# Output products of a gated feed-forward kernel: h as the stationary operand and the output weights as the streamed one

## The chip, the cores and the metric

One core of a Trainium2 chip runs the kernel. The metric is the device time of one execution in microseconds (us). Its engines are TensorE (PE, matrix products; its weight loads are listed apart as PEld), VectorE (DVE), ScalarE (ACT), GpSimd (POOL) and SyncE (SP, which here only issues DMAs).

## The reference

Two stages follow each other. The first is a causal convolution over 7 taps whose weights are a softmax and differ by token and head; the second is a gated feed-forward layer. Tokens: 4 x 4096; channels: 192 in 8 heads of 24; hidden width: 1536.

```python
w = softmax(weight_gen, axis=-1)                      # (4, 4096, 8, 7)
x_unf = windows of 7 tokens of x, zeros ahead         # (4, 4096, 7, 8, 24)
x = einsum('bshk,bskhg->bshg', w, x_unf).reshape(16384, 192)
gate = 1 / (1 + exp(-(x @ w_gate)))                   # 192 -> 1536
out = (gate * (x @ w_val)) @ w_out                    # 1536 -> 192, float32
```

## The kernel before

**Precision.** PE works on fp32r operands, which hold fewer bits than fp32. Each operand is therefore kept as a rounded part and a rest: W as hi and lo, h as hh and hl, the convolved x as two planes. A product is made of three: hi x hi, lo x hi and hi x lo.

**Tiling.** The 16,384 tokens are 32 blocks (n) of 512. The hidden width is 12 slices (f) of 128. A *unit* is one slice of one block. The first slices of blocks 0 and 1 are cut into two units of 256 tokens (table `APART`), so that PE can begin with half a block.

**PE's order.** The array is split into an upper and a lower half of 64 rows (`UP`, `LOW`), which run two matmuls beside each other; a product that contracts 128 or 192 channels is made of such halves. A unit's period (`period`) has 14 slots, each one matmul of 512 columns in the lower half paired with one in the upper half. Gate (lower half, 9 matmuls, `G`) and value (upper half, 9, `V`) belong to unit s. The output products (`out_jobs`: 5 matmuls in each half) belong to the unit three periods earlier (`LAG`); the upper half makes its five in slots 2 to 6, the lower half in slots 9 to 13. The output weights are stationary and h streams, 512 tokens at a time: three products for output channels 0 to 127 into one bank (`ph`), two for channels 128 to 191, hi and lo side by side as 128 columns, into another (`pt`). `ph` and `pt` have two banks each, which alternate between blocks; gate and value have the other four of the eight PSUM banks. The output leaves transposed, channels by tokens, and is turned on the host side of the return.

**Turns.** Both halves add into the same bank, one after the other. Where a bank passes from one half to the other, `emit` puts a GpSimd memset of one cell (`seen`) between the last matmul of one and the first of the other.

**Other engines in a unit.** ACT takes the sigmoid of the gate (L1050), DVE multiplies by the value (L1053), ACT rounds h to hh (L1056), DVE subtracts for hl (L1059). At the end of a block `evac` copies `ph` (ACT, L1108), copies the upper half of `pt` (ACT, L1111), adds it to the lower half (DVE, L1114) and stores both (SP).

**Opening.** Nothing can be multiplied before the first softmax, the spreading of its weights over partitions (L637), the tap products (DVE, L796) and their sum. For the first half block, the heads of the second half block and those of block 1's first half, that sum is made on PE by an identity matrix (L718, table `SUMS`), elsewhere on DVE (L704). ACT then rounds (L826, L872), DVE subtracts for the rest (L829, L875), and ACT copies the halves crosswise (`As`, `T`). The weights of each slice are loaded, put together and split by `convert`: ACT, DVE, ACT, then two DVE subtractions (L472). Units of blocks 0 and 1 alternate in turns of six slices: block 0, f 0 to 5; block 1, f 0 to 5; block 0, f 6 to 11; block 1, f 6 to 11.

**The order.** All operations are recorded with a modelled duration, a due time and the buffers that they take; a list scheduler (`Plan.order`) sets the order on each engine. Its first operations are not planned but listed by number (`FIRST`). Engines then run their queues in order and wait by semaphores. Where the plan sees PE idle early on, matmuls on a blank tile are put in (`idle`, `between`).

Of the kernel before, what the change touches and what calls it, by code (L numbers as in the profile page):

```python
# [62 lines left out]
class Plan:  # L63
# [26 lines left out]
    def op(self, engs, fn, deps=(), alloc=(), uses=(), due=INF, table=None, nbytes=0, late=0.0, after=(), lag=None, port=True, more=0.0, lead=0.0, hold=None, tail=0.0):  # L90
# [12 lines left out]
        o.name = name  # L103
# [27 lines left out]
    def order(self):  # L131
# [17 lines left out]
        table, dma_free = None, 0.0  # L149
# [11 lines left out]
        def slots(o):  # L161

            got, when = [], 0.0
            for p, _ in o.alloc:
                best = None
                for b in self.places[p]:
# [104 lines left out]
def conv_gated_ffn(ctx: ExitStack, tc: tile.TileContext, xt, wg, wcat, outT):  # L271
# [30 lines left out]
    SUMS = {(0, 0): ("ph", "pt"), (0, M2): ("ph", None), (1, 0): ("ph", None)}  # L302
    APART = {0: (4, HALVES), 1: (3, HALVES)}
# [31 lines left out]
    place("ev", 2, [P, N], F32)  # L335
    place("osb", 2, [P, N], F32)
# [3 lines left out]
    for name, a, z in (("gv", 0, 4), ("ph", 4, 6), ("pt", 6, 8)):  # L340
        plan.place(name, [bank[:, i, :] for i in range(a, z)])
# [36 lines left out]
    LAG, SKIP = 3, 0  # L378
# [14 lines left out]
    def out_unit(s):  # L393

        if s < SKIP:
            return s - LAG + 1
        return s - LAG if s > SKIP else -1

    def out_period(u):
        return u + LAG - 1 if u + LAG - 1 < SKIP else u + LAG  # L400

    for s in range(len(units) + LAG):
        for i, slots in enumerate((2, 5, 2, 5) if out_unit(s) >= 0 else (0, 0, 9, 0)):
            _, _, a, z = units[min(s, len(units) - 1)]
            t += slots * slot(z - a)
            due[s, i] = t

    def due_block(n):
        return due[out_period(last_unit[n]), 3]
# [29 lines left out]
    LO = CT + R  # L439
    conv_op, selected = {}, {}  # L440

    def convert(f, due=INF):
# [4 lines left out]
        def ld(buf, e):  # L447
# [6 lines left out]
            {"sp": SP}, ld, [selected.get(f)], after=[prev.get("ld")], nbytes=P * CT * 8 * RAW, due=due  # L454
# [15 lines left out]
        def lows(a, z, to):  # L470
            def f_lo(buf, e):
                nc.vector.tensor_tensor(  # L472
                    out=W[f][:, to : to + z - a], in0=buf[E][:, a:z],
                    in1=W[f][:, a:z].bitcast(F32), op=ALU.subtract,
                )

            return f_lo

        o_top = op({"act": act(CT) + 0.06}, f_top, [o_ld], alloc=[("ch", X)])
        o_va = op({"dve": dve(CT) + 0.035}, f_value, [o_ld, o_top], alloc=[("ce", E)], uses=[X])  # L480
        o_hi = op({"act": act(CT)}, f_hi, [o_va], uses=[E])
        o_lo = [
            op({"dve": dve(z - a)}, lows(a, z, to), [o_hi], uses=[E])
            for a, z, to in ((0, CB + P, LO), (CB + P, CT, CT))
        ]
        conv_op[f] = dict(ld=o_ld, done=[o_hi] + o_lo)


# [743 lines left out]
```

## Time and profile before

| | us |
|---|---|
| median of 3 runs | 1255.74 (1255.38 to 1256.42) |
| profiled execution | 1255.93 |
| its span, first to last instruction | 1254.2 |
| PE busy | 1244.5 (99%) |
| PE weight loads busy | 1103.6 (88%) |
| DVE busy | 976.5 (78%) |
| ACT busy | 597.0 (48%) |
| POOL busy | 135.2 (11%) |

Busy times are unions over the span; of matmuls that overlap, as pairs on the two halves of the array do, each has its own duration in the tables of groups. A matmul's listed duration holds the time in which its last column drains, so the step from one start to the next, not the duration, says what it costs a full queue. Register, branch, semaphore and DMA-issuing instructions are not counted as busy.

### The profile page before, as it was taken

Reading aid. Unit: us, or ns where it says so; the run is one execution under the profiler, and the core shown is the slowest. Engines: PE = TensorE matmul, PEld = TensorE weight load, DVE = VectorE, ACT = ScalarE, POOL = GpSimd, SP = SyncE. Lnnn points to the kernel's source line nnn. Section 1 sums busy time; section 2 is a strip of 40 time slices with the busy share of each in tenths; the row PEclk is TensorE's granted clock in tenths of the full one; section 3 lists DMA queues with packets and bytes.
Section 4 is the critical chain, followed back from the end, with each engine's and each line's share of the span. In section 5 each row is a group of like instructions: output and inputs, shape, how many; then the busy total and the mean of one; then the engine's idle time right before and its main releaser. Section 6 shows DMA issues by size and latency. Waiting matters only on the chain.

```text
span 1254.2 us, 29144 instructions
## 1 busy us (share of the span) xinstructions
PE 1244.5 (99%) x11047; PEld 1103.6 (88%) x11047; DVE 976.5 (78%) x1444; ACT 597.0 (48%) x1016; POOL 135.2 (11%) x1498
## 2 busy tenths in 40 slices
PE   8999999999999999999999999999999999999998
PEld 7988888888888888888888888888888888888887
DVE  8999998898977688776778767688676887767743
ACT  6866555554534444444444444444344444444443
POOL 0111111111111111111111111111111111111110
PEclk9999999999999999999999999999999999999999
DMA  9765539445272743529344282652727335293100
GB/s 252 234 160 131 140 85 230 116 120 140 72 176 72 175 105 82 127 71 202 77 118 110 63 197 73 140 121 58 168 72 182 97 80 129 72 204 75 39 14 14
DMA packets 48988, 150.33 MB, mean 120 GB/s; under 512 B 6544, under 2 KB 19280, under 8 KB 48848
## 3 DMA queue, kind: packets, MB, share of 16 engines
q1 hardware_dynamic: 48704, 148.22, 49.0%
q8 instruction: 86, 1.41, 0.5%
q14 instruction: 54, 0.44, 0.1%
q10 hardware_dynamic: 144, 0.26, 0.1%
HBM read 110.24 MB, written 16.20 MB: 101 GB/s over the span
## 4 chain that ended last, share of the span: by engine, by line
PE 97%; DVE 1%; DMA 1%; issue 0%; ACT 0%; SPq 0%
PE bank L971 97%; PE bank L718 1%; DMA wb<-ws 1%; DMA ws<-w 0%; DVE prod L770 0%; DVE sg L1053 0%; DVE prod L704 0%; DVE hl L1059 0%; DVE m L516 0%; DVE eye L600 0%; DVE w L523 0%; DVE osb L1114 0%; DVE sel L605 0%; DVE W L472 0%; SPq L663 0%
## 5 line engine op out<-in xcount | busy, mean ns | idle before, releaser
L971 PE MATMUL bank<-hh,W 64*128 64x512 f32 (+2 forms) x2337 | 769.5, 383 | 0.0
L971 PE MATMUL bank<-As,W 64*128 64x512 f32 (+1 forms) x2346 | 646.5, 383 | 0.0
L971 PE MATMUL bank<-T,W 64*128 64x512 f32 (+1 forms) x2346 | 645.8, 382 | 0.0
L971 PE MATMUL bank<-hl,W 64*128 64x512 f32 (+1 forms) x1558 | 594.4, 382 | 0.2 <-DVE hl L1059 0.2
L971 PE MATMUL bank<-A,W 64*128 64x512 f32 (+1 forms) x2346 | 479.8, 382 | 0.0
L1056 ACT CAST hh<-sg 128x512 fp32r<-128x512 f32 (+1 forms) x391 | 239.9, 614 | 490.7 <-DVE sg L1053 490.4
L971 PEld LDWEIGHTS bank<-hh,W 64*128 64x128 f32 (+1 forms) x2337 | 428.5, 184 | 29.9 <-POOL seen L967 0.4
L971 PEld LDWEIGHTS bank<-T,W 64*128 64x128 f32 x2346 | 426.8, 184 | 29.6 <-ACT T L895 0.3
L971 PEld LDWEIGHTS bank<-As,W 64*128 64x128 f32 x2346 | 427.1, 184 | 29.2
L1053 DVE TENSOR_TENSOR sg<-bank,sg 128x512 f32<-128x512 f32 (+1 forms) x391 | 265.1, 678 | 168.1 <-PE bank L971 167.9
L1059 DVE TENSOR_TENSOR hl<-sg,hh 128x512 fp32r<-128x512 f32 (+1 forms) x391 | 265.4, 679 | 97.0 <-ACT hh L1056 94.5
L971 PEld LDWEIGHTS bank<-A,W 64*128 64x128 f32 x2346 | 298.3, 184 | 30.0 <-issue 0.3
L971 PEld LDWEIGHTS bank<-hl,W 64*128 64x128 f32 x1558 | 286.8, 184 | 20.0 <-DVE hl L1059 0.4
L1050 ACT ACTIVATE sg<-bank 128x512 f32<-128x512 f32 (+1 forms) x391 | 231.5, 592 | 116.0 <-PE bank L971 112.4
L967 POOL MEMSET seen<- 1x1 f32 x1490 | 133.5, 90 | 1110.2 <-PE bank L971 1108.1
L770 DVE TENSOR_TENSOR prod<-x,wb 128x1024 f32<-128x1024 f32 x126 | 136.4, 1084 | 0.9 <-DMA wb<-ws 0.7
L704 DVE TENSOR_TENSOR prod<-prod,prod 128x1024 f32<-128x1024 f32 (+2 forms) x94 | 104.2, 1109 | 0.0
L770 DVE TENSOR_TENSOR prod<-xt,wt 128x1024 f32<-128x1024 f32 (+1 forms) x66 | 68.7, 1042 | 0.0
L704 DVE TENSOR_TENSOR acc<-prod 128x512 f32<-128x512 f32 (+2 forms) x64 | 34.3, 536 | 0.1
L826 ACT CAST A<-acc 128x512 fp32r<-128x512 f32 (+1 forms) x31 | 19.0, 612 | 17.8 <-DVE acc L704 17.8
L1114 DVE TENSOR_TENSOR osb<-bank,ev 64x512 f32<-64x512 f32 x32 | 21.5, 671 | 1.4 <-ACT ev L1111 1.4
L704 DVE TENSOR_TENSOR prod<-prod 128x512 f32<-128x512 f32 (+1 forms) x34 | 22.5, 661 | 0.0
(52 smaller groups left out, 307.5 us busy)
## 6 DMA issues: line engine op xcount, KB each, us to landing
wb<-ws SPq DMA_DIRECT2D x60, 896.0 KB, 11.9
wt<-ws SPq DMA_DIRECT2D x30, 896.0 KB, 8.9
As<-A SPq DMA_DIRECT2D x56, 256.0 KB, 3.7
out<-osb SPq DMA_DIRECT2D x31, 256.0 KB, 2.4
x<-in_x SPq DMA_DIRECT2D x30, 259.0 KB, 9.5
T<-T SPq DMA_DIRECT2D x56, 128.0 KB, 4.1
raw<-in_w SPq DMA_DIRECT2D x12, 575.8 KB, 6.0
out<-osb SPq DMA_DIRECT2D x32, 128.0 KB, 2.5
```

Of the source, the lines that this page charges most:

```text
L704: nc.vector.tensor_tensor(out=dst(buf), in0=a(buf), in1=b(buf), op=ALU.add)
L718: nc.tensor.matmul(out(buf), eye, flat(buf, i, j - k, j - k + 1), start=j == 0, stop=j == K - 1,)
L770: nc.vector.tensor_tensor(out=dst.rearrange("p (k j t) -> p k j t", k=z - k, t=L), in0=sliding(buf[X][:, k : k + cols], z - k, [[L, cols / ...
L826: nc.scalar.copy(buf[A][:, 0, all_], buf[ACC][:, :C])
L967: turn = nc.gpsimd.memset(seen, 0.0)
L971: ins = nc.tensor.matmul(buf[dst][:, c:d], w, m, start=start, stop=stop)
L1050: nc.scalar.activation(out=buf[k["sg"]][:, a:z], in_=buf[k["g"]][:, a:z], func=AF.Sigmoid)
L1053: nc.vector.tensor_tensor(out=buf[k["sg"]][:, a:z], in0=buf[k["v"]][:, a:z], in1=buf[k["sg"]][:, a:z], op=ALU.mult)
L1056: nc.scalar.copy(buf[k["hh"]][:, a:z], buf[k["sg"]][:, a:z])
L1059: ENG[e].tensor_tensor(out=buf[k["hl"]][:, a:z], in0=buf[k["sg"]][:, a:z], in1=buf[k["hh"]][:, a:z].bitcast(F32), op=ALU.subtract)
L1114: nc.vector.tensor_tensor(out=buf[OT][LOW, :N], in0=buf[PT][LOW, :N], in1=buf[EV][LOW, :N], op=ALU.add)
```

## The change

Output products: h is now the stationary operand, 128 tokens at a time, and the output weights stream. For each 128 tokens (j = 0 to 3) and each half, hh is multiplied by hi and lo side by side (2 x 192 = 384 columns) and hl by hi (192 columns). One bank for each j (`po`) takes the sums, channels of hi in its first 192 columns and of lo in the next. All four banks belong to one block at a time. The two halves' matmuls are listed in the order of their modelled starts (`streams`) instead of in pairs; in the upper half output products follow 4 of the value's matmuls (`HEAD`), in the lower half all 9 of the gate's.

At a block's end ACT copies each bank's 384 columns, DVE adds hi and lo columns of all four in one operation, and one DMA stores tokens by channels. The last block is copied, added and stored bank by bank.

Around it: the slices of blocks 0 and 1 are no longer taken in turns; block 0 is in halves for f 0 to 5, block 1 for f 0 to 3. Only block 0's sums are made on PE. Where they are, PE also takes the rest (a product with a negative identity, `f_rest`), and ACT rounds it, instead of a DVE subtraction; for the heads and tail of block 0's second half, PE makes the crosswise turn too (`f_turn`). Each tap of a PE sum is an operation of its own. The weights' lo part is one DVE subtraction of 576 columns instead of two. Units 0 and 1 make their products with A and As before unit 0 makes those with T. `FIRST` is a new and longer list (its numbers are left out here).

```diff
-    LAG, SKIP = 3, 0
+    LAG, HEAD = 3, 4
-    SUMS = {(0, 0): ("ph", "pt"), (0, M2): ("ph", None), (1, 0): ("ph", None)}
-    APART = {0: (4, HALVES), 1: (3, HALVES)}
+    SUMS = {(0, 0): ("po", "po"), (0, M2): ("po", None)}
+    APART = {0: (6, HALVES), 1: (4, HALVES)}
+    TURNS = {(0, M2)}
...
-    place("ev", 2, [P, N], F32)
-    place("osb", 2, [P, N], F32)
+    place("ev", 1, [P, N // P, 2 * D], F32)
-    for name, a, z in (("gv", 0, 4), ("ph", 4, 6), ("pt", 6, 8)):
+    for name, a, z in (("gv", 0, 4), ("po", 4, 8)):
...
-    TURN = 6
-    spans = [(n, f, g) for f, g in ((0, TURN), (TURN, NF)) for n in range(2)]
-    for n, first, end in spans + [(n, 0, NF) for n in range(2, NB)]:
+    for n in range(NB):
         apart, cuts_ = parts(n)
-        units += [(n, f, a, z) for a, z in cuts_ for f in range(first, min(apart, end))]
-        units += [(n, f, 0, N) for f in range(max(first, apart), end)]
+        units += [(n, f, a, z) for a, z in cuts_ for f in range(apart)]
+        units += [(n, f, 0, N) for f in range(apart, NF)]
...
+            def f_rest(buf, e):
+                nc.tensor.matmul(
+                    buf[ACC][:, :n_], minus, buf[X][:, 0, here], start=False, stop=True, skip_group_check=True
+                )
...
+                if summed:
+                    nc.scalar.copy(buf[X][:, 1, here], buf[ACC][:, :n_])
+                else:
+                    nc.vector.tensor_tensor(
+                        out=buf[X][:, 1, here], in0=buf[ACC][:, :n_],
+                        in1=buf[X][:, 0, here].bitcast(F32), op=ALU.subtract,
+                    )
...
+                def f_turn(buf, e):
+                    opened.append(buf[B])
+                    nc.tensor.matmul(
+                        buf[B][:, :W2], turn_, buf[X][:, :, here], start=True, stop=True
+                    )
...
-    def out_jobs(u, r, head_first, last=False):
+    def out_jobs(u, r, last=False):
...
+        for j in range(a // P, z // P):
+            jobs.append((k["po"][j], (f, 2, j), k["hh"], rows, None, (0, 2 * D), f == 0 and r == 1, False))
+            jobs.append((k["po"][j], (f, 1, j), k["hl"], rows, None, (0, D), False, last))
...
+                if dst[0] == "po":
+                    f_, parts_, j = w
+                    w = buf[t][rows, j * P : (j + 1) * P]
+                    m = W[f_][rows].rearrange("p (w c) -> p w c", w=2)[:, :parts_, CB:]
+                    if parts_ == 1:
+                        m = m[:, 0]
...
+    def streams(low, up):
+        tops, out = [0.0, 0.0], []
+        todo = [list(low), list(up)]
+        while todo[0] or todo[1]:
+            i = 0 if not todo[1] or (todo[0] and tops[0] <= tops[1]) else 1
+            job = todo[i].pop(0)
+            out.append((tops[i], job))
+            tops[i] += cost(job)
+        return out, max(tops)
...
+            jobs, took = streams(G + low, V[:HEAD] + up + V[HEAD:])
...
+            if not fo:
+                cuts_ += [at[j[1:4]] for j in up[2::2]]
             if last:
-                evac(no, [c])
+                cuts_ += [at[j[1:4]] + 1 for j in low[1::2]]
...
+                    alloc=([("gv", g) for g in gv] if not i else []) + [("po", d) for d in new],
...
+            def f_copy(buf, e, j=j, PO=PO):
+                nc.scalar.copy(buf[EV][:, j], buf[PO][:, : 2 * D])
...
+            o = op(
+                {"act": act(D if end else 2 * D, True) + 0.12}, f_low if end else f_copy, [d], alloc=alloc,
+                uses=[PO] + ([EV] if j else []), after=copies[-1:], due=t - 4 + j if not end else t, lag=1,
+            )
...
+        if not end:
+            store(slice(0, N // P), [add(slice(0, N // P), copies)], "sp")
...
+    for s in range(2):
+        period(s, (0, 1))
     for s in range(len(units)):
-        period(s)
+        period(s, (2,) if s < 2 else (0, 1, 2))
```

## Rows read from the trace of the kernel before

**Rows 1.** The page, its first part: busy us (share of the span) xinstructions.
```profile
PE 1244.5 (99%) x11047; PEld 1103.6 (88%) x11047; DVE 976.5 (78%) x1444; ACT 597.0 (48%) x1016; POOL 135.2 (11%) x1498
```

**Rows 2.** Chain that ended last, in order of time: start us, us, what.
```profile
27.02 3.22 PE bank L718 x14
...
45.42 1203.58 PE bank L971 x10636
```

**Rows 3.** Timeline, steady stretch: start us, us, engine line operation out<-in.
```profile
700.03 0.63 PE L971 MATMUL bank<-A,W 64*128 64x512 f32 x4
...
700.49 0.39 PE L971 MATMUL bank<-As,W 64*128 64x512 f32 x1
700.49 0.18 PEld L971 LDWEIGHTS bank<-As,W 64*128 64x128 f32 x1
...
706.38 0.63 PE L971 MATMUL bank<-A,W 64*128 64x512 f32 x4
```

**Rows 4.** Busy time by stretch; last three columns: PE clock, DMA share, GB/s.
```profile
0.00:50.00 50.00, 44.87 (x430) 41.12 (x432) 45.47 (x96) 35.69 (x81) 4.96 (x44) 1.00 0.89 254
...
300.00:500.00 200.00, 200.00 (x1768) 177.07 (x1766) 156.40 (x226) 92.42 (x153) 21.50 (x240) 1.00 0.47 111
```

**Rows 5.** Timeline of weight loads, opening; xcount loads in one piece.
```profile
8.30 0.97 PEld L637 LDWEIGHTS bank<-w,sel 128*128 128x128 f32 x8 [0.90 <-DVE w L573]
...
17.18 1.64 PEld L718 LDWEIGHTS bank<-prod,eye 128*128 128x128 f32 x14 [0.83 <-DVE prod L796]
...
26.95 2.89 PEld L718 LDWEIGHTS bank<-prod,eye 128*128 128x128 f32 x14
```

**Rows 6.** Timeline where PE starts again after a wait.
```profile
44.95 0.42 DVE L1059 TENSOR_TENSOR hl<-sg,hh 128x256 fp32r<-128x256 f32 x1
...
45.42 0.18 PEld L971 LDWEIGHTS bank<-hl,W 64*128 64x128 f32 x1 [0.42 <-DVE hl L1059]
...
45.42 0.18 PEld L971 LDWEIGHTS bank<-As,W 64*128 64x128 f32 x1
...
45.53 0.19 PEld L971 LDWEIGHTS bank<-hh,W 64*128 64x128 f32 x1
45.53 0.19 PEld L971 LDWEIGHTS bank<-T,W 64*128 64x128 f32 x1
```

**Rows 7.** Timeline of half-array products with 256 columns, upper half.
```profile
30.75 0.28 PE L971 MATMUL bank<-hl,W 64*128 64x256 f32 x1
...
30.87 0.28 PE L971 MATMUL bank<-hh,W 64*128 64x256 f32 x1
```

**Rows 8.** Groups by line: xcount | busy us, mean ns | idle before.
```profile
L967 POOL MEMSET seen<- 1x1 f32 x1490 | 133.5, 90 | 1110.2 <-PE bank L971 1108.1
...
L1056 ACT CAST hh<-sg 128x512 fp32r<-128x512 f32 x377 | 234.3, 621 | 488.5 <-DVE sg L1053 488.4
L1050 ACT ACTIVATE sg<-bank 128x512 f32<-128x512 f32 x377 | 226.2, 600 | 115.4 <-PE bank L971 111.9
L1108 ACT COPY osb<-bank 128x512 f32<-128x512 f32 x32 | 18.8, 587 | 0.6
...
L826 ACT CAST A<-bank 128x256 fp32r<-128x256 f32 x3 | 1.1, 371 | 1.8 <-PE bank L718 1.8
...
L704 DVE TENSOR_TENSOR prod<-prod,prod 128x768 f32<-128x768 f32 x31 | 29.5, 951 | 0.0
```

**Rows 9.** Timeline of one turn: the last product and GpSimd's write.
```profile
301.57 0.39 PE L971 MATMUL bank<-hl,W 64*128 64x512 f32 x1
...
302.08 0.09 POOL L967 MEMSET seen<- 1x1 f32 x1 [0.36 <-PE bank L971]
```

**Rows 10.** Timeline of the opening, ACT, DVE and PE.
```profile
15.46 0.37 ACT L826 CAST A<-bank 128x256 fp32r<-128x256 f32 x1 [0.63 <-PE bank L718]
...
17.51 0.42 DVE L829 TENSOR_TENSOR A<-bank,A 128x256 fp32r<-128x256 f32 x1
...
18.94 0.62 PE L971 MATMUL bank<-A,W 64*128 64x256 f32 x6
```

More of the change, by code (lines that the diff above doesn't have):

```diff
@@ L88, in place, with op @@
         self.places[name] = [dict(buf=b, key=None) for b in bufs]
-    def op(self, engs, fn, deps=(), alloc=(), uses=(), due=INF, table=None, nbytes=0, late=0.0, after=(), lag=None, port=True, more=0.0, lead=0.0, hold=None, tail=0.0):
+    def op(self, engs, fn, deps=(), alloc=(), uses=(), due=INF, table=None, nbytes=0, late=0.0, after=(), lag=None, port=True, more=0.0, lead=0.0, hold=None, tail=0.0, fixed=False):
         keys = [k for _, k in alloc] + list(uses)
@@ L408, in due_block @@
     def due_block(n):
-        return due[out_period(last_unit[n]), 3]
+        return due[last_unit[n] + LAG, 3]
     x_op = {}
@@ L627, in idle, with spread @@
             )
-    def spread(key, chunks, sel, deps):
-        keys_ = [(key, i) for i in range(chunks // 2)]
+    def spread(key, chunks, sel, half):
+        keys_ = [(key, half, i) for i in range(chunks // 2)]
+        deps = [soft[0]["spread"][half]]
         def f(buf, e):
@@ L996, in conv_gated_ffn, with cost, pe, period @@
     u_op = {}
-    def pe(slots, deps, **kw):
+    def cost(job):
+        return slot(job[5][1] - job[5][0])
+    def pe(jobs, deps, took=None, **kw):
         last_pe[0] = op(
-            {"pe": sum(slot(max(j[5][1] - j[5][0] for j in p if j)) for p in slots)}, emit(slots), deps + [last_pe[0]], **kw
+            {"pe": sum(map(cost, jobs)) if took is None else took}, emit(jobs), deps + [last_pe[0]], **kw
         )
         return last_pe[0]
-    def period(s):
+    def streams(low, up):
[7 more added lines that the diff above has]
+        return out, max(tops)
+    def period(s, which=(0, 1, 2)):
         u = out_unit(s)
@@ L1025, in period @@
                 b.fill = between(s, not i)
+            if 2 not in which:
+                return
         else:
             last = fo == NF - 1
[L1028 to L1031 removed]
+            up, low = out_jobs(u, 1), out_jobs(u, 0, last)
             gv = [k["g"], k["v"]]
[L1033 to L1036 removed]
@@ new lines, in period @@
+            done = {}
+            for i, (x, y) in enumerate(zip(cuts_, cuts_[1:])):
+                part = [j for _, j in jobs[x:y]]
+                mine = [j[0] for j in part if j[0][0] == "po"]
+                mine = list(dict.fromkeys(mine))
+                new = [j[0] for j in part if j[0][0] == "po" and j[6]]
+                o = pe(
+                    part, deps if not i else conv_op[fo]["done"] + u_op[u] if x == at[up[0][1:4]] else [],
+                    time[i + 1] - time[i],
+                    alloc=([("gv", g) for g in gv] if not i else []) + [("po", d) for d in new],
+                    uses=xs + (gv if i else []) + [d for d in mine if d not in new] + ([ko["hh"], ko["hl"]] if mine else []),
+                    due=due[s, 0 if not i else 1 if x < at[low[0][1:4]] else 3],
+                )
+                if i < 2:
+                    o.fill = between(s, not i)
+                if y == at[low[0][1:4]]:
+                    b = o
+                for d in mine:
+                    done[d] = o
@@ L1049, in f_sig @@
+            c = o
+            if last:
+                evac(no, [done[po(j)] for j in range(N // P)])
         def f_sig(buf, e):
@@ L1072, in ending @@
     def ending():
-        three = range(len(units) - LAG, len(units))
-        ks = [keys(u) for u in three]
-        po = [ks[0]["ph"], ks[0]["pt"]]
-        used = [[k["hh"], k["hl"]] for k in ks]
-        def jobs(u, part, stop=False):
-            out = out_jobs(u, 0, True)
-            out = out[:3] if part == "ph" else out[3:]
-            out = [j[:3] + (slice(0, P),) + j[4:7] + (False,) for j in out]
-            if stop:
-                out[-1] = out[-1][:7] + (True,)
-            return [(j,) for j in out]
@@ L1087, in side @@
-        def side(jobs, deps, used, at):
-            return pe(jobs, deps, uses=po + used, due=due[len(units) + at, 3])
-        cf = sum((conv_op[units[u][1]]["done"] for u in three), [])
-        x, y, z = three
-        side(
-            sum((jobs(u, part) for u in (x, y) for part in ("ph", "pt")), []),
-            cf + u_op[x] + u_op[y], used[0] + used[1], 1,
-        )
-        t = jobs(z, "pt", True)
-        side(t[:1], u_op[z][:1], used[2], 2)
-        t = side(t[1:], u_op[z], used[2], 2)
@@ new lines, in ending, with side @@
+        x, y, z = range(len(units) - LAG, len(units))
+        ks = [keys(u) for u in (x, y, z)]
+        po = ks[0]["po"]
+        cf = sum((conv_op[units[u][1]]["done"] for u in (x, y, z)), [])
+        def side(jobs, deps, u, at):
+            return pe(jobs, deps, uses=po + [keys(v)[t] for v in u for t in ("hh", "hl")], due=due[len(units) + at, 3])
+        side(out_jobs(x, 2) + out_jobs(y, 2), cf + u_op[x] + u_op[y], (x, y), 1)
+        jobs = out_jobs(z, 2, True)
+        side(jobs[0:3:2], u_op[z][:1], (z,), 2)
```

366 lines of the change are left out of this document (175 added, 191 removed), and 43 rows, old and new, of the table FIRST.

## The prediction

> **What bounds the kernel now.** I read first the page's busy times: TensorE (PE) is busy 99% of the span [rows 1]. Then the chain of waits in order of time: from 45.42 us one piece of PE work, 1203.58 us long, runs without a wait to the last block; before it stand pieces such as the PE sums at 27.02, behind it 5 us of copies and stores [rows 2]. So from 45 us on the time is the number of PE instructions times what each holds the array. The reader is to see that in the steady timeline: the same matmul returns at 700.03 and 706.38, which is two units, 28 slots of one product on each half of the array, so 226.8 ns a slot [rows 3]. The granted clock there is 1.00, the 2.4 GHz level [rows 4]; 512 columns at it are 213.3 ns, so 13.4 ns go to each product beside its columns. A unit (512 tokens, one of 12 slices) is 14 slots, 3.175 us. The second resource is VectorE (DVE): busy 45.47 of the first 50 us, 78% over all [rows 1, 4].
>
> The profiled execution took 1255.93 us (span 1254.2), 0.2 above the median 1255.74 of the runs. The sum is made against 1255.93.
>
> **1. Output products: the core of the change.** Removed per unit and half: 5 products of 512 columns, 5 x 226.8 = 1134 ns. Added: 4 of 384 and 4 of 192 columns. By columns and overhead alone they cost 4 x (160 + 13.4) + 4 x (80 + 13.4) = 1067 ns.
>
> But each of the eight brings weights of its own, and a load is not free. In the steady rows the load for a half's next product begins with the present product of that half (700.49 and 700.49), not earlier [rows 3]: one set waits while one streams. What a load needs is seen where streams are short: the 8 loads of the selection products (224 columns) take 0.97 us, less the last one's own 0.19 and over 7 steps 111 ns; the 14 loads of the 128-column sums take 1.64 us, in the same way 112 ns over 13 steps [rows 5]. The two differ in columns and in passes and agree in step, while the same sums with 256 columns step at (2.89 - 0.19 - 0.11)/12 = 216 ns, which is their stream. So I read 111 to 112 ns as the load's own step. Those loads fill the whole array; for half loads the trace has only restarts, where both halves load at 45.42 and again at 45.53, 0.11 apart and side by side [rows 6]. 512-column products (227 ns) and 256-column ones (0.12 us, [rows 7]) hide such a load; a 192-column product (93) does not. It then holds its half until the next weights are in.
>
> For the 192-column product I take 112 ns, from the nearest steady rows [rows 5]. Ends: 93 below (the load is hidden after all) and 120 above (the shortest spacing that any half-array stream shows, [rows 7]); 105 if the load follows the restart rather than the steady rows. With 112: 4 x (173.4 + 112) = 1142 ns against 1134, +7.6 ns a unit. 384 units less the three whose products are made at the end: 381 x 7.6 = **+2.9 us**. With 105: -7.8 us; with 120: +15.1 us; with 93.4: -25.5 us.
>
> A rule that speaks against this change stands in the Trainium skill, "TensorE: Matmul & The Clock Gate", section "LDWEIGHTS (loading the stationary operand)": a load costs its columns over 1.2 GHz, however many rows it has, so 106.7 ns here, an estimate from that page. The 0.11 us of [rows 6] agree, for half the rows too. By it alone the eight products would cost 1120 ns and the change would bring 5 us.
>
> Full and half units: the lists cut 10 pairs of halves instead of 7, but output products no longer pay for a cut: three pairs more cost 3 x 18 x 120 - 3 x 9 x 227 = +0.36 us, and 7 x 10 x 120 - 7 x 5 x 227 = 0.46 us go. **-0.1 us.**
>
> **2. Turns.** When a bank passes from one half of the array to the other, GpSimd writes a cell in between. Turns double, from 4 to 8 a unit (1490 memsets of 90 ns now [rows 8]); 3,000 are 270 us of an engine that is 89% idle. On the path: a product begun at 301.57 (0.39 long) is answered at 302.08 and released at 302.17, 0.60 after its start [rows 9]. In the new order the upper half ends with bank 0 at 4 slots + 0.173 = 1.08 us, a shorter product, so it is released by 1.68; the lower half loads for that bank at 8 slots, 1.81. Both sides then step alike. **0**, with 0.13 us of cover; each 0.1 us that a turn came later than that would cost 38 us over the kernel, and below nothing there is nothing, for the turns cost nothing now.
>
> **3. One set of banks.** Today two blocks' sums alternate and the evacuation has 38 us. Now the first product of a block waits for ScalarE (ACT) to copy the same bank. Four copies of 384 columns: 512 columns take 587 ns and 256 take 371 [rows 8], so 480 each, 1.92 us. In the period that ends a block: the gate's last product begins at slot 8, ends at 1.81 + 0.39 = 2.20, the sigmoid (600 ns [rows 8]) follows 0.12 later, as the turn's write does [rows 9], to 2.92, the copies end at 4.84 at the earliest, and hand over some 0.04 later (hl ends at 45.37, its load starts 45.42, [rows 6]). The next block's load for bank 3 is due one period (3.18), 4 slots (0.91), two banks (0.57) and one 384 stream (0.17) on: 4.83. So bank 3 is late by 0.05 us; banks 0 to 2 have 0.09 to 0.6. Queued behind the waiting load are the products of both halves. 31 boundaries: 1.6 us. Other ACT work between the copies (a cast of 621 ns [rows 8]) in one boundary of ten adds 1.9. **+3.5 us**; ends 0 and 31 x 0.67 = 20.8.
>
> The DVE sum of a block becomes one of 768 columns, 951 ns [rows 8], beside PE, with DVE 22% idle; without that cover it would cost 30 us in all. One store instead of two leaves SP less to issue; its buffer is wanted again a block later.
>
> **4. Opening.** Two things go from the path. The rest of the first half block is now taken by PE and ACT: its cast ends at 15.83, but DVE comes to the subtraction only at 17.51 and the first products start at 18.94 behind the tail's sums [rows 10]; with one product and one cast of 0.4 they could start near 16.6, **-2.3**. And block 1's sums on PE go: 14 products, 3.22 us, on the chain at 27.02 [rows 2], **-3.2**. Against it: block 0 now takes all 12 slices first, so 5 conversions more are due before block 0 ends, each two DVE operations of 576 columns, by the 951 ns of 768 [rows 8] 1.4 us; the second half of block 1, some 5,400 columns or 6.7 us of DVE, is due later; and block 1's sums return to DVE, 1,536 columns or 1.9 us. SP's queue moves too: five weight loads of 128 x 576 x 8 bytes, 2.9 MB or 11.6 us at the 254 GB/s of the first 50 us [rows 4], come before that half's 1.5 MB. DVE and DMA (0.89 busy) are nearly full here, so some of the 5.5 is given back. I take **-3**, ends -6 (both kept) and +8 (five conversions late, 7).
>
> The end: 24 products at 285/2 on average, 3.4 us, for 15 at 0.23 [rows 3], 3.4 us; the last bank then needs a copy and a DVE sum of 192 columns, some 0.3 each, where now a copy of 0.59 stands [rows 8]. **0**, within 0.3.
>
> **Sum.** 1255.9 + 2.9 - 0.1 + 3.5 - 3.0 = **1259.2 us**, 3.5 above the median: slightly slower. The saved 3.6% of columns are eaten by the loads.
>
> **Rivals.**
> A. *The loads don't bind.* For it: no row shows a half-array product shorter than 256 columns, and the steps of [rows 5] are full-array ones. Against: restarts in halves show the same 0.11. Then -25.5; the shorter period makes bank 3 late by 0.18, 31 x 0.18 + 1.9 = 7.5; 1255.9 - 25.5 - 0.1 + 7.5 - 3 = **1234.8 us**.
> The Trainium skill, "TensorE: Matmul & The Clock Gate", section "Back-to-back issue gap", gives 81 ns as the sustained step of 128-column products with their loads; no row here shows a step that short, but by it A would hold.
> B. *A half-array load steps at 120*, with the 13.4 ns on top of the load as on top of the stream. For it: 0.12 in [rows 7] may already be the load. Against: 226.8 shows the same 13 ns with no load near. The slower period takes bank 3's lateness away: 1255.9 + 15.1 - 0.1 + 1.9 - 3 = **1269.8 us**.
> C. *The evacuation becomes the bound at block edges*: a 621 ns cast stands between the copies at every edge. For it: ACT runs in order, and the cast to hh comes once a period. Against: copies are due earlier in the plan. It decides once ACT gives the four copies more than 1.9 us. 1255.9 + 2.9 - 0.1 + 20.8 - 3 = **1276.5 us**.
>
> **Chances.** Forecast 0.50, A 0.24, B 0.13, C 0.13. What can be told from no change is about 0.2%, 2.5 us: 1253.2 to 1258.3. Of the forecast's half, 0.22 is slower than that (its terms as they stand), 0.20 within (an opening that gains 5), 0.08 faster (with loads at 105 as well). So faster 0.32, same 0.20, slower 0.48. The forecast's own range is 1250 to 1267. The range that leaves 2 in 10 out takes in A's middle and most of B and C: 1233 to 1275.
>
> **What will show it.** In a steady stretch, the step from a 192-column product to the next one of its half: 112 ns (mine), 93 (A), 120 (B); the unit's period 3.18, 3.11 or 3.21 us. Load busy time rises well above 88%. At block edges a PE wait for an ACT copy of 0.05 us on bank 3, or 0.6 (C). In the opening, first products near 16.6 us. I am wrong if the period is under 3.15 us, or if PE waits for GpSimd in steady units.

## The result: 1.3% slower, by a term that the sum did not have

The changed kernel takes 1272.22 us (median of 4 runs, 1271.9 to 1272.73) against 1256.08 on the same chip before (4 runs); the ratio is 1.0128, 95% interval 1.011 to 1.0145. The profiled execution took 1272.3 us, span 1270.5; before it was 1255.93 and 1254.2. The direction was forecast, the size was not: +16.4 us where the sum had +3.3.

The page after, its first part, against [rows 1]: busy us, share, instructions. Weight loads went from 88% to 98%, GpSimd's turns doubled, and PE stayed full.

```profile
PE 1263.9 (99%) x13327; PEld 1244.3 (98%) x13327; DVE 991.3 (78%) x1441; ACT 607.0 (48%) x1086; POOL 259.7 (20%) x2932
```

The chain of waits after, against [rows 2]: start us, us, what. The first main products begin at 16.27 in this chain (forecast 16.6). L629 are PE's filling products, five pieces of 0.2 to 0.4 us behind 16 us, in which PE in truth waits. The last piece is one run of main products, as before.

```profile
16.27 0.55 PE bank L1001 x6
...
18.23 0.41 PE bank L629 x2
...
72.38 1193.72 PE bank L1001 x10301
```

So the time must lie inside that run. The length of a unit shows it: the start of the sigmoid of one unit to that of the next. ACT's timeline after, at the end of the kernel, where one unit follows another undisturbed: four units in 12.88 us, 3.220 each.

```profile
1249.21 0.60 ACT L1112 ACTIVATE sg<-bank 128x512 f32<-128x512 f32 x1 [0.73 <-PE bank L1001]
...
1262.09 0.60 ACT L1112 ACTIVATE sg<-bank 128x512 f32<-128x512 f32 x1 [0.72 <-PE bank L1001]
```

Before, ACT's timeline has 20 units in 63.47 us, and over 320 units (216.61 to 1232.07 us) they take 3.1733 each.

```profile
660.87 0.60 ACT L1050 ACTIVATE sg<-bank 128x512 f32<-128x512 f32 x1 [0.47 <-PE bank L971]
...
724.34 0.60 ACT L1050 ACTIVATE sg<-bank 128x512 f32<-128x512 f32 x1 [0.47 <-PE bank L971]
```

The difference of 46.7 ns times 384 units is +17.9 us. The rest is -0.6 us at the opening (the steady run, carried back to its first unit, starts at 25.6 instead of 26.2) and -1.0 at the end (from the last full unit's sigmoid to the span's end 8.42 instead of 9.38 us). Together +16.3, the difference of the spans.

Which products got longer? PE's timeline after, rows of both halves of the array mixed. One half runs the output products (hh 703.99, 704.27, 704.55: a pair of 384 and 192 columns every 0.285 us), then from 704.84 its main products of 512 columns: 0.25 (the first still waits for the weights of the last short one), 0.23, 0.23, 0.24.

```profile
703.99 0.35 PE L1001 MATMUL bank<-W,hh 64*128 64x384 f32 x1
...
704.18 0.25 PE L1001 MATMUL bank<-W,hl 64*128 64x192 f32 x1
704.27 0.35 PE L1001 MATMUL bank<-W,hh 64*128 64x384 f32 x1
...
704.55 0.36 PE L1001 MATMUL bank<-W,hh 64*128 64x384 f32 x1
...
704.78 0.33 PE L1001 MATMUL bank<-W,hh 64*128 64x384 f32 x1
704.84 0.41 PE L1001 MATMUL bank<-As,W 64*128 64x512 f32 x1
...
705.09 0.39 PE L1001 MATMUL bank<-As,W 64*128 64x512 f32 x1
...
705.32 0.39 PE L1001 MATMUL bank<-T,W 64*128 64x512 f32 x1
...
705.55 0.39 PE L1001 MATMUL bank<-T,W 64*128 64x512 f32 x1
705.79 0.38 PE L1001 MATMUL bank<-T,W 64*128 64x512 f32 x1
```

The step that the prediction named as its sign needs care. By the starts of the products a 192-column product is followed after 88 ns (704.18 to 704.27), below even Rival A's 93, and a 384-column product after 197. But a 384-column product behind a short one is listed some 20 ns longer (0.35 or 0.36 us) than one behind 512 columns (the other half's at 704.78, 0.33): it begins before its weights are in and waits. So the loads tell the step, and the pair is 285 ns, where Rival A needs 267.

The weight loads after, same stretch: after a 384-column product's load at 704.18 the next one of that half starts 0.11 us later, and so at 704.96 and 705.07. That is the 192-column product, held by the next load. From the starts in nanoseconds it is 108; the load after that follows 176 ns later.

```profile
704.18 0.18 PEld L1001 LDWEIGHTS bank<-W,hh 64*128 64x128 f32 x1
704.29 0.19 PEld L1001 LDWEIGHTS bank<-W,hl 64*128 64x128 f32 x1
...
704.96 0.18 PEld L1001 LDWEIGHTS bank<-W,hh 64*128 64x128 f32 x1
705.07 0.19 PEld L1001 LDWEIGHTS bank<-W,hl 64*128 64x128 f32 x1
```

The same rows by their starts in ns, as steps from one product of a half to its next (my differences):

```
before, any steady stretch:  227 227 226 227 227 226 ...            (mean 226.67)
after, the nine of a unit:   254 229 233 236 224 231 236 228 233    (254 holds 22 ns of the last short one)
```

Nine products of 512 columns take 2080 ns instead of 2040, 40 more. The eight output products take 4 x 284.9 = 1139.4 ns instead of 5 x 226.67 = 1133.3, 6 more. These 46 ns are the unit's whole growth. The output products are what the sum said; the gate and value products, which the change does not touch, carry the loss.

### The profile page after: what moved, and what is told of

It is laid out like the page before. It is cut to its first block, busy times and chain, and to the rows that moved or that the text cites. A ratio compares the mean times of both kernels' runs of the same rounds, so it can differ in the third digit from the quotient of the medians.

```text
span 1270.5 us, 36599 instructions
## 1 busy us (share of the span) xinstructions
PE 1263.9 (99%) x13327; PEld 1244.3 (98%) x13327; DVE 991.3 (78%) x1441; ACT 607.0 (48%) x1086; POOL 259.7 (20%) x2932
## 4 chain that ended last, share of the span: by engine, by line
PE 98%; DMA 0%; DVE 0%; ACT 0%; SPq 0%; issue 0%; DVEq 0%
PE bank L1001 98%; DMA xt<-in_x 0%; PE bank L724 0%; PE bank L629 0%; ACT L1225 0%; SPq L453 0%; DVE m L539 0%; DVE ev L1181 0%; PE bank L871 0%; DVE ce L465 0%; DVE prod L801 0%; ACT sel L614 0%; ACT w L530 0%; DVE w L552 0%; DVE m L548 0%
## 5 line engine op out<-in xcount | busy, mean ns | idle before, releaser
L1001 PE MATMUL bank<-W,hh 64*128 64x384 f32 x3060 | 873.5, 351 | 0.0
L1001 PE MATMUL bank<-W,hl 64*128 64x192 f32 x3060 | 745.8, 247 | 0.0
L1001 PE MATMUL bank<-As,W 64*128 64x512 f32 (+1 forms) x2364 | 579.8, 388 | 0.0
L1001 PEld LDWEIGHTS bank<-W,hl 64*128 64x128 f32 x3060 | 570.3, 187 | 2.0
L1001 PEld LDWEIGHTS bank<-W,hh 64*128 64x128 f32 x3060 | 535.3, 184 | 4.6 <-issue 0.2
L989 POOL MEMSET seen<- 1x1 f32 x2924 | 257.9, 88 | 1003.1 <-PE bank L1001 899.8
L1001 PE MATMUL bank<-A,W 64*128 64x512 f32 (+1 forms) x2364 | 366.0, 388 | 0.0
L1001 PEld LDWEIGHTS bank<-As,W 64*128 64x128 f32 x2364 | 349.7, 185 | 5.5
L1001 PEld LDWEIGHTS bank<-A,W 64*128 64x128 f32 x2364 | 248.4, 185 | 4.1 <-ACT sg L1112 0.4
L1178 ACT COPY ev<-bank 128x384 f32<-128x384 f32 x124 | 50.5, 497 | 1.8 <-PE bank L1001 1.8
```

Source lines behind the costliest of these rows:

```text
L989: turn = nc.gpsimd.memset(seen, 0.0)
L1001: ins = nc.tensor.matmul(buf[dst][:, c:d], w, m, start=start, stop=stop)
L1178: nc.scalar.copy(buf[EV][:, j], buf[PO][:, : 2 * D])
```

## The experiments

Each ran beside the kernel before on the same chip, once unless a number of runs is given; the lengths of units and steps are read inside the traces. First: do the two halves, now out of step, hold each other up?

**The halves shifted, before and after.** A product of zeros with 448 columns was added to the upper half at every 30th unit, so that the offset between the halves changes by 200 ns each time.

```diff
+    SHIFTS = range(60, 370, 30)
...
+            if s in SHIFTS:
+                first_two[0] += ((k["v"], "zero", k["A"], UP, None, (a, a + 448), False, False),)
```

> The kernel before, with one product of a zero weight tile with 448 columns (some 200 ns) put into the upper half alone, at every 30th unit from 60 to 360. Nothing else changes, so each shifts the upper half against the lower by 200 ns, or by 27 less than a slot of 227, and eleven of them go once round the slot. Theory P (halves out of step cost time: 512-column products take 231 ns instead of 227 when the halves don't start together): the unit's period, 3.173 us with the halves 17 ns apart, rises to as much as 3.173 + 14 x 0.0044 = 3.235 us in most stretches between two shifts and comes back near 3.173 where the offset is small again; in all some 8 x 30 x 0.06 + 2 = 16 us more, about 1272 us. Rival Q (a product is slowed by the many short products and loads of the other half, not by the offset): 3.173 us in every stretch, and about 1258 us for the shifts themselves.

Measured: 1259.35 us (before 1258.35); the unit has 3.1733 us in every stretch.

> The changed kernel with the same eleven shifts of the upper half. P: the period differs by stretch; where the gate and value products of the two halves start together, the 9 products of 512 columns are back at 227 ns and the period near 3.18 us, elsewhere 3.22. Q: 3.22 us in every stretch, whatever the offset.

Measured: 1275.78 us, 3.220 to 3.222 us a unit at every offset (one stretch reads 3.149 between sigmoids, but there ACT was late at its start). The offset has no influence on the unit: the theory is out.

**Both output products 288 columns.** The sum of columns is the same, but no product is shorter than its successor's load; the columns are others than wanted.

```diff
-                    m = W[f_][rows].rearrange("p (w c) -> p w c", w=2)[:, :parts_, CB:]
+                    m, d = W[f_][rows, CT : CT + 288], 288
...
```

> The changed kernel, but both output products of 128 tokens stream 288 columns of the weights' lo part instead of 384 (hi and lo) and 192 (hi): the same number of columns and loads, other values, so the output products are not the reference's. Theory L (a load takes 108 ns of its half and a 192-column stream does not cover it): 288 columns are 120 ns and cover it, so each pair costs 2 x (120 + 13 to 18) = 267 to 276 instead of 285 ns, the unit 34 to 72 ns less, 3.15 to 3.19 us, and the kernel 1246 to 1259 us. Rival (only the number of columns and of products counts, and each product costs some 18 ns beside its columns): period 3.22 and 1272 us as in the changed kernel.

Measured: 1239.14 us (before 1258.35), 33 less than the changed kernel and more than expected. PE's timeline of this run, one half: a pair takes 0.27 and 0.26 us (mean 263 ns) where it took 285.

```profile
699.80 0.29 PE L999 MATMUL bank<-W,hh 64*128 64x288 f32 x1
...
699.93 0.29 PE L999 MATMUL bank<-W,hl 64*128 64x288 f32 x1
700.07 0.29 PE L999 MATMUL bank<-W,hh 64*128 64x288 f32 x1
...
700.33 0.29 PE L999 MATMUL bank<-W,hh 64*128 64x288 f32 x1
```

4 x 22 ns x 381 = 33 us. So the load of the weights is what holds a 192-column product, as forecast; and since the 512-column products still take 231 ns on average here, with no product shorter than a load, the load is not what slows those.

**One shorter product in the kernel before.** What is left is the mix of lengths itself. In the opening of before, where 256 and 512 columns meet, the 512s take 225 to 236 ns too. So one of the 14 products of a half and unit was cut to 448 columns: once where the other half's neighbour in the list is another product, once in the same slot of both halves.

```diff
+                    if dst[0] == "pt" and t[0] == "hl" and d - c == N:
+                        d -= 64
```

> The kernel before, with one of the 14 products of each half and unit (the last 64 output columns' product with the low part of h) streaming 448 columns instead of 512; 64 columns of that product are left out. It has less work than before. Theory T (a half's 512-column products take 226.67 ns only in a row of equal lengths, and about 231 ns after any change of length, as in the opening of before at 57 to 66 us): 13 x 231 + 200 = 3.203 us a unit instead of 3.173, so about 380 x 0.03 = 11 us longer, some 1268 us. Theory F (a product costs its columns and a fixed 13.4 ns, whatever stands beside it): 3.173 - 64/2.4 ns = 3.147 us a unit, 10 us shorter, some 1247 us.

> The kernel before, with the second of the 14 products in both halves of the array streaming 448 columns instead of 512 (64 columns of it are left out). Unlike in e4_before_448 the short product stands in the same slot in both halves, so that the halves stay in step and the order of the list is the order in which they run. Theory T (any change of length unsettles the 512-column products): about 3.20 us a unit, some 1268 us, as e4. Theory O (the 512-column products of the changed kernel are late because the halves' steps differ in length and PE's one list holds one half for the other): 3.147 us a unit, some 1247 us, whatever e4 gives. Theory F (columns and a constant): 1247 us too.

Measured: 1253.88 and 1253.85 us (before 1257.19), 3.1667 us a unit in both: 6.7 ns less where the columns alone give 26.7. Neither expectation met the number. PE's timeline of the first run shows why: behind the 448 columns at 700.59 come steps of 0.23, 0.23, 0.24, 0.23 (in ns 236, 228, 233, 231, over 236 units the same within 0.5), then 226.67 for the other nine.

```profile
700.59 0.36 PE L973 MATMUL bank<-hl,W 64*128 64x448 f32 x1
...
700.79 0.39 PE L973 MATMUL bank<-A,W 64*128 64x512 f32 x1
...
701.02 0.39 PE L973 MATMUL bank<-As,W 64*128 64x512 f32 x1
...
701.25 0.39 PE L973 MATMUL bank<-As,W 64*128 64x512 f32 x1
...
701.49 0.39 PE L973 MATMUL bank<-As,W 64*128 64x512 f32 x1
...
701.72 0.39 PE L973 MATMUL bank<-T,W 64*128 64x512 f32 x1
```

A half that has changed its length loses 21 ns over four products and then settles; its other products stay at 226.67 while the other half goes through its own four. It does so in the same slot of both halves as well, so neither their step nor the list's order makes it.

**All 17 products 512 columns.** The changed kernel, its eight output products widened, other columns than wanted; from unit 40 on the list is sorted by these equal lengths.

```diff
-                    m = W[f_][rows].rearrange("p (w c) -> p w c", w=2)[:, :parts_, CB:]
+                    m, d = W[f_][rows, CT : CT + N], N
...
```

> The changed kernel with all 8 output products of a half and unit streaming 512 columns of the low part of the weights instead of 384 and 192 (other columns than the reference wants, so its output is not the reference's); from unit 40 on the list is sorted by these equal lengths. All 17 products of a half and unit are then equally long. Theory T: 17 x 226.67 = 3.853 us a unit, the steps regular at 226 and 227 ns; 1272 + 381 x 0.633 = some 1513 us. Theory X (something else of the changed kernel makes its 512-column products 231 ns: its list, its four banks, weights as the moving side): 17 x 231 = 3.927 us, some 1541 us, the steps between 224 and 236 ns.

Measured: 1518.24 us, 3.8533 us a unit in most stretches, which is 17 x 226.67. Weights as the moving side, the four banks and the turns cost the products nothing here.

**The list sorted by measured times.** In `streams`, the time by which the two halves' products are merged became 231.1, 175.5 and 109.4 ns.

> The changed kernel, the same products, with the list of the two halves sorted from unit 40 on by measured durations (231.1, 175.5 and 109.4 ns for 512, 384 and 192 columns) instead of columns + 32 at 2.4 GHz; it exchanges one or two neighbours per unit. Theory T: no change, 3.220 us a unit, some 1272 us. Theory O (one half waits in the list behind the other's later product): the 40 ns per unit that its 512-column products lose come back wholly or in good part, 3.18 to 3.20 us a unit, 1257 to 1265 us.

Measured: 1272.69 us, 3.220 us a unit. The order of the list is not it.

**What a row follows, in before.** Ten lengths of the short product, each for 30 units.

```diff
+                    if dst[0] == "gv" and t[0] == "A" and w[1] >= LO and dst[1] in LENGTHS:
+                        d = c + LENGTHS[dst[1]]
...
```

> The kernel before with the second product of both halves shortened (columns left out), by stretches of 30 units: 508, 496, 480, 416, 384, 320, 256, 192, 128 and 64 columns instead of 512. With 448 (e6) the unit took 3.1667 us: 26.7 ns less work, 20 ns more for the next four products. Theory T2: in each stretch the 13 others begin with a few uneven steps and settle at 226.67, so that the period is 3.1733 - (512 - n)/2.4 ns + a loss between 0 and 40 ns that depends on n and does not grow with 512 - n; stretches of few columns less are longer than before or equal to it (508: up to 3.21). From 192 columns down the next product's weights hold the short one at 108 ns, as in the changed kernel: 3.055 us and the same loss for 192, 128 and 64. Rival W2 (the loss is a fixed 20 ns for any change): 3.192, 3.187, 3.180, 3.153, 3.140, 3.113, 3.087, then 3.075 us. The whole some 1235 to 1245 us.

Measured: 1243.11 us (before 1256.4). ACT's timeline of this run, 20 units with 496 columns and 20 with 480: 63.34 us and 64.13. With less to do, the unit got longer, 3.2066 against 3.1667 us, and longer than before's 3.1733.

```profile
313.14 0.60 ACT L1056 ACTIVATE sg<-bank 128x512 f32<-128x512 f32 x1 [0.46 <-PE bank L973]
...
376.48 0.60 ACT L1056 ACTIVATE sg<-bank 128x512 f32<-128x512 f32 x1
...
408.41 0.60 ACT L1056 ACTIVATE sg<-bank 128x512 f32<-128x512 f32 x1 [0.22 <-PE bank L973]
...
472.54 0.60 ACT L1056 ACTIVATE sg<-bank 128x512 f32<-128x512 f32 x1 [0.49 <-PE bank L973]
```

By length: the undisturbed unit, the same by columns alone, and the steps of the 512s behind the short product (median over the stretch, ns; my differences of starts; 448 is the second run of the pair above):

```
columns  us a unit  by columns  the 512s that follow
  508     3.1867     3.1717     232 233 231 227 227 ...
  496     3.1667     3.1667     227 227 227 ...
  480     3.2066     3.1600     235 233 236 224 231 236 228 233 231 227 ...
  448     3.1667     3.1467     236 228 233 231 227 ...
  416     3.1466     3.1333     232 232 231 227 ...
  384     3.1466     3.1200     231 231 236 228 232 231 227 ...
  320     3.1000     3.0933     233 231 226 227 ...
  256     3.0867     3.0667     232 236 228 232 231 227 ...
```

But for a row's first step, which can be off by some nanoseconds, there is one sequence, 235 233 236 224 231 236 228 233 231, and then 226.67 for good. What went before sets where a row enters it: at once settled (496), four from the end (448), or at its beginning (480, 47 ns lost). A fixed price per change of length is ruled out. From 192 columns down the weights bind: the loads behind the short product start 108 ns apart, whatever its length. The unit has 3.060 us with 192 columns, where the row is settled at once, and 3.087 with 128 and with 64, where five uneven steps follow (231 236 228 233 231). The one loss for all three that was expected is not there.

**Longer rows in the changed kernel.** Six more products of 512 columns (zeros) per half and unit.

```diff
+                G = G[:1] + [(gv[0], "zero", k["A"], LOW, None, (a, z), False, False)] * 6 + G[1:]
...
```

> The changed kernel with six more products of 512 columns (zero weights) per half and unit from unit 60 on, so that a row of equal lengths has 15 instead of 9 products between the output products of one unit and those of the next. Theory T2 (the row settles, but later than the ninth product): the steps go on from 228, 233 with at most one or two more uneven ones, then 226.67 to the end of the row; the six cost 6 x 226.67 + 4 to 10 ns, 4.584 to 4.590 us a unit. Rival X2 (products of this kernel never settle, whatever the row's length): all at 231.1, 3.220 + 6 x 0.2311 = 4.607 us a unit. 1272 + 325 x 1.365 = some 1716 us by the one, 325 x 1.387, some 1723 us by the other.

Measured: 1747.51 us, over both numbers. But the rows settle: 253 (22 of it the last short one) 229 234 235 225 230 236 229 232 231, then 227 226 227 227 226, and an undisturbed unit has 4.580 us. PE's timeline of this run, the end of such a row:

```profile
285.38 0.39 PE L1003 MATMUL bank<-A,W 64*128 64x512 f32 x1
...
285.60 0.39 PE L1003 MATMUL bank<-A,W 64*128 64x512 f32 x1
...
285.83 0.39 PE L1003 MATMUL bank<-As,W 64*128 64x512 f32 x1
...
286.06 0.33 PE L1003 MATMUL bank<-W,hh 64*128 64x384 f32 x1
```

That is 1.360 more than in the changed kernel. The expectation counted 325 units; 334 carry the zeros, 1272 + 454 = 1726 us. Most of the 21 us beyond is this experiment's own: at block edges PE waits for the copies of the banks (waits: engine line, what for, us in total, times, longest).

```profile
PEld bank L1003 <- ACT ev L1183: 18.1, 28, 6.9
```

So a row behind this kernel's output products has ten uneven steps before it settles, one more than the longest of the table. The changed kernel's own row ends with the ninth product, one before that.

**Four of 384, then four of 192.**

```diff
+            if s >= 40 and fo and not last:
+                up, low = up[::2] + up[1::2], low[::2] + low[1::2]
```

> The changed kernel with the eight output products of a half and unit in another order: the four of 384 columns, then the four of 192 (from unit 40 on, the first and last unit of a block left as they are). Same work, and lengths change three times per half and unit instead of nine. e4 showed that after one short product the next four of 512 columns start 236, 228, 233 and 231 ns apart and then 226.67 (21 ns lost), while in the changed kernel all nine of a unit go on at 229, 233, 236, 224, 231, 236, 228, 233. Theory T2 (a row of 512-column products needs some 4 to 10 products to settle, how many depends on the products that went before it): the row begins otherwise and loses another sum, 0 to 40 ns a unit, 3.18 to 3.22 us, 1257 to 1272 us. Rival V (the last change, 192 to 512, alone sets the steps): the same steps as in the changed kernel, 3.22 us, 1272 us. Rival W (every change costs some nanoseconds of its own): 40 x 3/9 = 13 ns instead of 40, 3.193 us, 1262 us.

Measured: 1367.66 us; no theory had it. A new wait: with all four hl products at the end, the lower half asks for its banks soon after the upper has left them. The timeline of this run has GpSimd's four writes together at 704.42 and a load behind them, and PE's loads wait for them 313 times, 89.3 us in all.

```profile
704.42 0.53 POOL L989 MEMSET seen<- 1x1 f32 x4 [1.79 <-PE bank L1001]
704.56 0.18 PEld L1001 LDWEIGHTS bank<-W,hh 64*128 64x128 f32 x1 [0.32 <-POOL seen L989]
```

Where no wait breaks them, rows here go through steps of the same sequence, so the run does not tell the theories apart. But it prices the turns when their cover is gone: 3.487 us a unit on average (units 60 to 380), 0.27 more than in the changed kernel.

**What a row follows, in the changed kernel.** Three orders of the pairs, then seven widths of the last short product.

```diff
+    for i, o_ in enumerate(((1, 0, 3, 2, 5, 4, 7, 6), (0, 1, 3, 2, 4, 5, 7, 6), (1, 0, 2, 3, 5, 4, 6, 7))):
...
+    for i, d_ in enumerate((224, 240, 256, 272, 288, 304, 320)):
```

> The changed kernel; what stands directly before a row of nine 512-column products is varied by stretches of 30 units (first and last units of blocks keep their order). Units 60 to 89: the 192 columns before the 384 in each of the four pairs, so that a row follows a product of 384 columns; 90 to 119: every second pair so (384 192, 192 384, ...); 120 to 149: the others. From unit 150 the last product of 192 columns of each half streams 224, 240, 256, 272, 288, 304 and 320 columns of the low part of the weights instead (other columns than the reference wants, so the output is not the reference's). Theory T2 (a row goes through the sequence 235 233 236 224 231 236 228 233 231 before it stays at 226.67, and what it follows sets where it enters; shown in before by e9 for single short products): 224 columns (106.7 ns, still hidden by the 108 ns of the next weights) change nothing, 3.220 us; 240 to 320 cost 5 to 39 ns of columns and the row's loss goes to anything from 0 to 47 ns instead of 40, so that the period leaves the line 3.220 + (n + 32) / 2.4 - 108 ns by up to 40 ns downwards in some stretches, where the rows show few uneven steps; so do one or more of the three orders (3.18 to 3.22, without added columns). Rival V (the rows of this kernel always lose 40 ns): the periods stand on that line, 3.220, 3.225, 3.232, 3.239, 3.245, 3.252 and 3.259, and the orders give 3.220. Whole: 1265 to 1278 us.

Measured: 1272.72 us (before 1255.42). By widths undisturbed units have 3.220, 3.200, 3.207, 3.240, 3.247, 3.247, 3.240: 224 columns change nothing; 240 and 256, 5 and 12 ns more to stream, make the unit 20 and 13 ns shorter. By orders they have 3.207, 3.173 and 3.193. ACT's timeline of this run, four units in the second order (12.69 us, 3.173 each) and 20 at 240 columns (64.04 us, a slower first unit of a block among them):

```profile
328.27 0.60 ACT L1123 ACTIVATE sg<-bank 128x512 f32<-128x512 f32 x1 [0.42 <-PE bank L1004]
...
340.96 0.60 ACT L1123 ACTIVATE sg<-bank 128x512 f32<-128x512 f32 x1 [0.71 <-PE bank L1004]
...
594.11 0.60 ACT L1123 ACTIVATE sg<-bank 128x512 f32<-128x512 f32 x1 [0.75 <-PE bank L1004]
...
658.15 0.60 ACT L1123 ACTIVATE sg<-bank 128x512 f32<-128x512 f32 x1 [0.79 <-PE bank L1004]
```

**That order everywhere.** 384 192, 192 384, 384 192, 192 384 from unit 40 on, but for a block's first unit, which must open its banks with the 384. Nothing is left out.

```diff
+            swap_ = j % 2 and f and r < 2 and u >= 40
...
+            jobs += pair[::-1] if swap_ else pair
```

> The changed kernel with the order that did best in e11 (units 90 to 119) from unit 40 on, in all units but the first of a block: 384 192, 192 384, 384 192, 192 384, so that lengths change five times instead of nine per half and unit and a row follows a product of 384 columns. Nothing is left out. e11's undisturbed units of that order have 3.173 us, as before. Theory T2: 344 units x 11/12 x 46.7 ns = 14.7 us less than the changed kernel, some 1257.5 us, ratio to before 1.000 to 1.003: the loss in the rows was the change's whole cost, and what stays is the first units of the blocks (1.3 us) and the first 40 units (1.9 us) against 1.6 us won at the opening and the end. Rival V (rows always lose 40 ns, e11's stretch a coincidence of its neighbours): 1272 us, 1.013.

Measured: 1257.69 us, median of 11 runs (1257.24 to 1258.42), against 1256.67 before (15 runs): ratio 1.0009, 95% interval 0.9999 to 1.0018. Expected 1257.5. PE's timeline of this run: behind the short products the row is settled from its first step on, 0.23, 0.23, 0.22, 0.23, 0.22 (226 or 227 ns).

```profile
720.39 0.39 PE L1005 MATMUL bank<-As,W 64*128 64x512 f32 x1
...
720.62 0.39 PE L1005 MATMUL bank<-As,W 64*128 64x512 f32 x1
...
720.85 0.39 PE L1005 MATMUL bank<-T,W 64*128 64x512 f32 x1
...
721.07 0.39 PE L1005 MATMUL bank<-T,W 64*128 64x512 f32 x1
...
721.30 0.39 PE L1005 MATMUL bank<-T,W 64*128 64x512 f32 x1
...
721.52 0.85 PE L1005 MATMUL bank<-A,W 64*128 64x512 f32 x6
```

The same 34 products per unit in another order give some 14.5 us back. By the steps, 40 of the 46 ns come back in the rows (nine at 226.67) and 5 in the output products, whose eight now take 1134 ns instead of 1139. That is the missing term, shown. The order does not beat the kernel before.

## Why the forecast was right in direction and short in size

- **What bounds it**: right. From 16 us on PE has hardly a wait.
- **Output products, +7.6 ns a unit**: right, +6. The short product is held by the next weights for 108 ns (112 taken from [rows 5], 0.11 in [rows 6]); its neighbour takes 176. Rival A (93) and B (120) fall, though the unit of 3.220 us looks like B's sign (3.21). [rows 5] alone did not prove the load: the same sums step at 216 ns with 256 columns, so 128 columns stream some 108 ns as well, and the 224 columns of the selection products, priced as the prediction priced 192 and 384, take 107. The 288-column run proves it. The Trainium skill, "TensorE: Matmul & The Clock Gate", section "LDWEIGHTS (loading the stationary operand)", has 106.7 for such a load, an estimate from that page: the traces agree, with 64 rows too. The 81 ns of its section "Back-to-back issue gap" are in no row here: the loads of one half never start less than 108 ns apart in the stretches read.
- **"13.4 ns go to each product beside its columns"**: the step that failed. It was read off steady rows of one length [rows 3] and carried to a kernel of three. Measured: 231.1 ns for each 512-column product instead of 226.67, 9 x 4.4 = 40 ns a unit, 381 x 40 = 15.2 us. The rows that would have told lie in the trace of before, where half units meet full ones (below): one half has 512-column products at 64.20, 64.44, 64.67 and 64.91, 0.235 a step. The prediction used 256-column products only [rows 7].

```profile
64.20 0.39 PE L971 MATMUL bank<-As,W 64*128 64x512 f32 x1
...
64.44 0.39 PE L971 MATMUL bank<-As,W 64*128 64x512 f32 x1
...
64.67 0.39 PE L971 MATMUL bank<-T,W 64*128 64x512 f32 x1
...
64.91 0.38 PE L971 MATMUL bank<-T,W 64*128 64x512 f32 x1
```

- **Turns, 0**: right; PE's loads have no wait for GpSimd behind 76 us. The cover is real: without it the unit was 0.27 us longer.
- **One set of banks, +3.5**: 0. Behind 76 us PE waits for no copy, and the 1.9 us for other ACT work did not come either. The step added up the copies' listed times. One is listed with 497 ns (480 thought), but they overlap: the next one starts some 0.37 us after the last, and the 31 sets of four are busy for 50.5 us (the group below), 1.63 us a set instead of 1.92. So bank 3 is free some 0.3 us earlier than thought, and the unit of 3.22 us asks for it 0.04 later. Rival C falls.

The group of the copies after: xcount, busy us, mean ns, idle before.

```profile
L1178 ACT COPY ev<-bank 128x384 f32<-128x384 f32 x124 | 50.5, 497 | 1.8 <-PE bank L1001 1.8
```

- **Opening, -3**: -0.6. Both gains came (first products at 16.27; the 3.22 us of sums [rows 2] are off the path), and more was given back than thought. 1.7 us of it are the filling products; the rest is not taken apart.
- **End, 0**: -1.0.

With 2.3 (loads), 15.2 (rows), -0.6 and -1.0 the sum is 1255.9 + 15.9 = 1271.8; 1272.3 was measured. That the wide range of 1233 to 1275 us held the time is luck: it owes its upper part to rivals B and C, whose mechanisms did not occur, and the forecast's own range ended at 1267.

## What to carry to other kernels

An overhead per instruction that is read in a row of equal instructions holds for such a row: before pricing a change that mixes sizes, look for the stretch where the trace already mixes them, and read the untouched neighbours, not only the new products. When a product is shorter than its successor's weight load, price it by the load. When the sum of the new parts comes out right and the time does not, measure the parts that were not changed.

## What the runs showed of the hardware

A product of 512 columns (fp32r, half the array) starts 226.67 ns after its forerunner only in a settled row. After a product of another length a half goes through up to ten uneven steps, in the main those of 235 233 236 224 231 236 228 233 231, entered at different places; the loss was 0 to 47 ns, and 16 columns decided between nothing (496) and 47 (480). A product whose columns stream in less than the load of the next weights is held to 108 ns, from load to load (192 columns; half the array too). The granted clock was 1.00 in these stretches, the 2.4 GHz level. The sequence follows the half's own products: shifting the other half, or giving it the same short product at the same time, changed nothing. What inside the array makes the sequence, and how the entry follows from the lengths, stays open; no run here looked further.
